# A fused forgetting-attention and SiLU block: q and k loaded in larger pieces and turned as one block, x of three more batches turned by TensorE, outputs issued by ScalarE

## Chip, cores and metric

One core of a Trainium2 chip runs the whole program. The metric is device time in microseconds (us), lower is better. Engines are named as in the profile: PE (TensorE; PEld is its weight load), DVE (VectorE), ACT (ScalarE), POOL (GpSimd), SP (SyncE, which only issues DMAs here). A q behind a name (SPq) is the engine's queue of DMA issues. Lines (L130) are those of the kernel before.

## The reference

Eight batches, eight heads, 576 tokens, head dimension 64. Attention with a forget gate, then a block of two matmuls with SiLU between them on all 4608 tokens:

```
scores = q @ k.T / sqrt(64)                       # per batch and head, 576 x 576
cum    = cumsum(log(clip(f, 1e-4, 1)))            # per batch and head
attn   = softmax(where(causal, scores + cum[i] - cum[j], -1e9))
x      = (attn @ v), heads side by side           # 4608 x 512
h      = x @ w_in                                 # 4608 x 2048
out    = (h * sigmoid(h)) @ w_out                 # 4608 x 512
```

## The kernel before

Heads go in pairs p = 0 to 31, four pairs to a batch (batch b = p // 4). For a pair the kernel needs qT and kT (head dimension on partitions, tokens along the row) and `vaug`, v scaled by the decay, which POOL prepares (`prep_v`, L246). `scores` makes the score blocks of the causal triangle in four tiles (PE `sc`, L276), ACT takes their exponential into `uT` (L301), DVE multiplies the diagonal blocks by a mask (L315). `attend_rows` multiplies uT with vaug (PE `avr`, L344), and DVE normalises the result into `xt`, token by token (L353, L354). x must then be turned so that the model dimension lies on partitions: either by PE (`turn_pair`: five transposes `tpx`, L366, and ACT copies into `xT`, L372) or by DMA transposes (`turn_batch`, L377, issued by SP).

The second half goes in nine groups of 512 tokens. `m1_chunk` makes 128 rows of h for a group (four matmuls of 128x512, PE `hp`, L395), ACT takes a tanh (L406), DVE finishes SiLU into `gtile` (L407). `m2_part` makes a quarter of an output tile of 128 tokens (four matmuls, PE `po`, L420); after the fourth ACT copies the tile to `osb` (L429), and SP issues the DMA to `out` (L433). `osb` has two buffers. All results of attention transposes, attends, hp and po share four buffers of PSUM (`big`).

How q and k get turned depends on the batch. Batches 0 and 1: loaded as float32 (`whole`, `raw`), cast by POOL (`cast_main` L188, `cast_tail` L197) and turned by PE (`transposes`, L230), copied by DVE (L235, L239). Batches 2 to 7 (`NEARLY` is 2): `load_qk` (L121) is a DMA issued by POOL that casts to bf16 on its way, one for each block of 128 tokens (the last has 64) and each of q and k, 60 in all, in pieces of 64 elements; `turn_qk` (L130) is a DMA transpose for each, issued by SP, straight into qT or kT.

The order of every engine is the order of the calls (a manual schedule). The main loop goes over pairs 4 to 31. For a pair it runs the entries of `plan` (turns and v loads, all on SP), then the scores in two halves with m1/m2 work between them (`work(n)` takes chunks off two lists, alternating where both are allowed), `prep_v` of the next pair, the casts, the entries of `fetch` (loads on POOL), and the attend of the pair before. `pace` decides how much m1/m2 work goes into a pair, so that what is ready lasts until the next group becomes ready. A group is ready when x of all its tokens is turned: for batches 0 and 1 right after the last `turn_pair`, for the later ones `LAG` (12 us of planned PE time) after the last attend, since the DMA transposes take their time. `clock`, `spend` and `defer` are that planned time.

The weights are cast-loaded by POOL as well: w_in early (L567), w_out at L611, between the casts of pair 4 and those of pair 5. In POOL's order prep_v of pair 4 (L613) follows, which needs v of batch 1.

Of the kernel before, what the change touches and what calls it, by code (L numbers as in the profile page):

```python
# [13 lines left out]
BF16 = mybir.dt.bfloat16  # L14
P = 128
# [3 lines left out]
def kernel(  # L19
# [37 lines left out]
    w_out_bf = const.tile([P, NFC, DM], BF16, name="w_out_bf")  # L57
    NVA = 3
    vaugs = [const.tile([P, NB, 2, DV], BF16, name=f"vaug{i}") for i in range(NVA)]
    kTs = [const.tile([P, NPB, NB * P], BF16, name=f"kT{i}") for i in range(2)]  # L60
    us = [const.tile([P, 2, UW], BF16, name=f"uT{i}") for i in range(3)]

    xp = ctx.enter_context(tc.tile_pool(name="xp", bufs=4))
    qkp = ctx.enter_context(tc.tile_pool(name="qkp", bufs=2))
# [6 lines left out]
    tpool = ctx.enter_context(tc.tile_pool(name="tpool", bufs=3))  # L71
    opool = ctx.enter_context(tc.tile_pool(name="opool", bufs=2))
    NEARLY = 2
    LAG = 12.0
    MOST = 9.0
    HOLD = 6
    qkT: dict[int, tuple] = {}
# [1 line left out]
    raw: dict[tuple, bass.AP] = {}  # L79

    def qk_tiles(b):
        qkT[b] = (qkp.tile([P, NPB, S], BF16, name="qT", tag="qT"), kTs[b % 2])

    def raw_tile():
        return stp.tile([P, DM], FP32, name="raw", tag="raw")
# [29 lines left out]
            in_=v[b, :, c * P : c * P + bs[c], :].rearrange("h p d -> p h d"),  # L115
        )

    def load_qk(b, c, which):
        t = sbp.tile([P, DM], BF16, name="mp", tag="mp", bufs=20)
        raw[b, c, which] = t  # L120
        nc.gpsimd.dma_start(  # L121
            out=t[: bs[c], :].rearrange("p (h d) -> p h d", h=H),
            in_=(q, k)[which][b, :, c * P : c * P + bs[c], :].rearrange("h p d -> p h d"),
        )

    def turn_qk(b, c, which):
        if b not in qkT:
            qk_tiles(b)
        n = bs[c]
        nc.sync.dma_start_transpose(  # L130
            out=qkT[b][which][:, :, c * P : c * P + n], in_=raw[b, c, which][:n, :]
        )

    f_sb = evp.tile([BH, S], FP32, name="f_sb", tag="ev")

# [278 lines left out]
    def m2_part(g, tb, part):  # L414
        if part == 0:
            po_open[g, tb] = big([P, DM], FP32, "po")
        po, gte = po_open[g, tb], gtiles[g]
        n = NFC // 4
        for fc in range(part * n, (part + 1) * n):
            nc.tensor.matmul(  # L420
                po[:, :],
                lhsT=gte[:, fc, tb * P : (tb + 1) * P],
                rhs=w_out_bf[:, fc, :],
                start=(fc == 0),
                stop=(fc == NFC - 1),
            )
        if part == 3:
            osb = opool.tile([P, DM], FP32, name="osb", tag="osb")
            nc.scalar.activation(  # L429
                out=osb[:, :], in_=po[:, :], func=ACT.Copy, scale=0.5  # L430
            )
            t0 = g * TG + tb * P
            nc.sync.dma_start(out=out[t0 : t0 + P, :], in_=osb[:, :])  # L433

    m1_queue = [(g, fc) for g in range(NG) for fc in range(NFC)]
    m2_queue = [(g, tb, pt) for g in range(NG) for tb in range(4) for pt in range(4)]
# [42 lines left out]
    def pace(p):  # L479
        b, j = divmod(p, NPB)  # L480
        if b < NEARLY:
            return have() / (NPB - j)
        for b in range(B):
            if (b + 1) * S // TG > m1_ready:
                break
        n = MOST
        for _ in range(20):
            k = NPB * b + NPB - p + LAG / (2.3 + 0.88 * n)
            n = 0.5 * n + 0.5 * have() / max(k, 1.0)
        return min(n, MOST)  # L490

# [14 lines left out]
    plan: dict[int, list] = {}  # L506

    fetch: dict[int, list] = {}

    def add(to, at, fn, *args):  # L510
        to.setdefault(at, []).append(lambda: fn(*args))

    for b in range(NEARLY, B):
        for i, group in enumerate([(0, 1), (2,), (3, 4)]):
            at = NPB * b - 4 + min(i, 1) if b == NEARLY else NPB * b - 7 + i
            for c in group:
                for w in range(2):
                    add(fetch, at, load_qk, b, c, w)
                    add(plan, at + (2 if b == NEARLY else 3), turn_qk, b, c, w)
                add(plan, NPB * b - 5 + i + (b == NEARLY), load_v, b, c, nc.sync)  # L520

    def load_w(dst, src, c0, c1):
        nc.gpsimd.dma_start(
            out=dst[:, :, c0:c1], in_=src[:, c0:c1].rearrange("(c p) x -> p c x", p=P)
        )

    with tc.manual_schedule():
# [80 lines left out]
        turn_pair(NPB - 1)  # L608
        m1_ready = 1
        cast_both(NPB)  # L610
        load_w(w_out_bf, moe_w_out, 0, DM)  # L611
        cast_both(NPB + 1)
        prep_v(NPB)  # L613
        work(HOLD)
        transposes(NPB, 0)
        work(1)
# [3 lines left out]
        for p in range(NPB, NP):  # L620
            b, j = divmod(p, NPB)
            early = b < NEARLY
            for fn in plan.get(p, []):
                fn()
            due += pace(p)
            n = int(due)
            due -= n
            n1, n2 = (n + 2) // 3, (n + 1) // 3
            n3 = n - n1 - n2
            scores(p, 0)  # L630
            scores(p, 1)
            spend(0.4)
            work(n1)
            ahead = p + 1 < NPB * NEARLY
            rows = NPB < p < NPB * NEARLY
            if ahead:
                transposes(p + 1, 0)
            if rows:
                attend_rows(p - 1, LO)
                spend(0.6)  # L640
            if p + 1 < NP:
                prep_v(p + 1)
            if p + 2 < NPB * NEARLY:
# [64 lines left out]
```

## Time and profile before

| | us |
|---|---|
| median of 3 runs (374.92, 381.12, 383.23) | 381.12 |
| the profiled execution | 378.66 |
| its span, first to last instruction | 376.9 |

| engine | busy us | share of the span |
|---|---|---|
| PE | 339.6 | 90% |
| ACT | 208.4 | 55% |
| DVE | 189.7 | 50% |
| POOL | 118.3 | 31% |

A row of the page's part 5 gives line, engine, operation, tiles out<-in, shape and count, then busy time, mean ns of one, and the idle time of the engine just before such instructions with what ended it. These are the rows of the steps that the change touches:

```profile
L121 POOL DMA_DIRECT2D mp<-in_q_dram x30 | 26.7, 889 | 0.0
L121 POOL DMA_DIRECT2D mp<-in_k_dram x30 | 25.8, 862 | 1.3 <-PE tpx L366 1.3
L372 ACT COPY xT<-tpx 128x512 bf16<-128x512 bf16 (+3 forms) x16 | 5.6, 405 | 3.6 <-PE tpx L366 3.6
```

And part 6, the DMA issues, with the size of each and the median time from issue to landing:

```profile
out_dram<-osb SPq DMA_DIRECT2D x36, 256.0 KB, 2.3
vm<-in_v_dram SPq DMA_DIRECT2D x32, 256.0 KB, 5.6
mp<-in_q_dram POOLq DMA_DIRECT2D x24, 128.0 KB, 5.1
mp<-in_k_dram POOLq DMA_DIRECT2D x24, 128.0 KB, 6.8
w_out_bf<-in_moe_w_out_dram POOLq DMA_DIRECT2D x1, 2048.0 KB, 19.0
```

KB counts the side written for a casting load. A wait row names engine, operation and line, what it waited for, the total, how often and the longest. Share of DMA in the windows can exceed 1 where several packets are under way on an engine.

### The profile page before, as it was taken

How to read it: one execution, taken by the hardware profiler on the slowest of the kernel's cores; microseconds unless marked ns; L12 is line 12 of the kernel's file. 1: busy time of each engine (PE TensorE's matmuls, PEld its weight loads, DVE VectorE, ACT ScalarE, POOL GpSimd, SP SyncE). 2: the span in 40 equal slices, each digit the busy share in tenths (PEclk: the TensorE clock that was granted, in tenths of full speed). 3: DMA queues.
4: the chain of work that ended last, by engine and by line, in shares of the span. 5: the costliest groups of instructions: out<-in, count | busy, mean ns of one | idle time of the engine just before them, and what ended most of it. 6: DMA issues, size and time to landing. Idle time of an engine off the chain costs nothing.

```text
span 376.9 us, 6954 instructions
## 1 busy us (share of the span) xinstructions
PE 339.6 (90%) x2637; PEld 165.7 (44%) x2637; DVE 189.7 (50%) x442; ACT 208.4 (55%) x329; POOL 118.3 (31%) x201
## 2 busy tenths in 40 slices
PE   2898939973999975999999999999999999999996
PEld 1455415541455442444544454444444454444442
DVE  3765844430684355775646555355535641754310
ACT  4575742532874763866566656566656723643421
POOL 5644039868045549134333421111110000000000
PEclk9999987995999998999999999999999999999999
DMA  9999988999999999969999995450310023001012
GB/s 223 221 217 289 179 174 56 132 172 143 200 167 157 138 187 181 160 82 136 156 163 151 80 138 116 105 134 28 85 64 29 30 57 92 29 0 57 28 56 83
DMA packets 152993, 46.09 MB, mean 122 GB/s; under 512 B 141120, under 2 KB 147264, under 8 KB 152960
## 3 DMA queue, kind: packets, MB, share of 16 engines
q1 hardware_dynamic: 93504, 34.23, 45.1%
q0 software_dynamic: 59376, 11.28, 40.4%
q8 instruction: 20, 0.33, 0.4%
q14 instruction: 13, 0.11, 0.1%
q10 hardware_dynamic: 80, 0.15, 0.1%
HBM read 36.85 MB, written 9.44 MB: 123 GB/s over the span
## 4 chain that ended last, share of the span: by engine, by line
PE 71%; DMA 11%; SPq 9%; POOL 4%; ACT 2%; issue 2%; DVE 1%; POOLq 0%; ACTq 0%
PE po L420 31%; PE hp L395 29%; PE sc L276 5%; PE avr L344 5%; SPq L113 4%; DMA mp<-in_k_dram 4%; DMA qT<-mp 3%; DMA vm<-in_v_dram 3%; SPq L96 2%; SPq L130 2%; POOL vaug L246 1%; ACT th L406 1%; DMA whole<-in_k_dram 1%; POOL mp L121 1%; ACT uT L301 1%
## 5 line engine op out<-in xcount | busy, mean ns | idle before, releaser
L395 PE MATMUL hp<-xT,w_in_bf 128*128 128x512 bf16 x576 | 142.8, 385 | 1.3 <-ACT xT L372 0.7
L420 PE MATMUL po<-w_out_bf,gtile 128*128 128x512 bf16 x576 | 140.8, 381 | 0.0
L407 DVE SCALAR_TENSOR_TENSOR gtile<-th,hp 128x512 bf16<-128x512 bf16 x144 | 97.4, 686 | 74.8 <-ACT th L406 71.8
L406 ACT ACTIVATE th<-hp 128x512 bf16<-128x512 f32 x144 | 85.4, 605 | 73.5 <-PE hp L395 65.5
L301 ACT ACTIVATE uT<-sc 128x1024 bf16<-128x1024 f32 (+1 forms) x128 | 100.8, 842 | 45.6 <-PE sc L276 36.7
L246 POOL TENSOR_TENSOR vaug<-vm,wT 128x512 bf16<-128x512 f32 x64 | 45.4, 730 | 147.5 <-PE avr L344 126.3
L395 PEld LDWEIGHTS <-w_in_bf 128*128 128x128 bf16 x576 | 53.8, 99 | 66.1 <-issue 7.9
L420 PEld LDWEIGHTS <-gtile 128*128 128x128 bf16 x576 | 53.8, 98 | 63.6 <-issue 3.5
L315 DVE TENSOR_TENSOR uT<-uT,mask 128x256 bf16<-128x256 bf16 (+1 forms) x112 | 34.9, 332 | 72.1 <-ACT uT L301 71.7
L276 PE MATMUL sc<-qT,kT 64*128 64x64 bf16 (+4 forms) x384 | 38.6, 293 | 17.7 <-DMA qT<-mp 10.8
L429 ACT ACTIVATE osb<-po 128x512 f32<-128x512 f32 x36 | 21.7, 602 | 39.0 <-PE po L420 32.4
L344 PE MATMUL avr<-vaug,uT 128*128 128x65 bf16 x960 | 36.5, 195 | 0.7 <-DVE uT L315 0.7
L344 PEld LDWEIGHTS <-uT 128*128 128x128 bf16 x960 | 33.9, 99 | 7.3 <-DVE uT L315 0.8
L276 PEld LDWEIGHTS <-kT 64*128 64x128 bf16 x384 | 15.3, 96 | 46.7 <-issue 32.2
L354 DVE TENSOR_TENSOR xt<-avr,rr 128x384 bf16<-128x384 f32 x64 | 31.4, 491 | 2.4
L121 POOL DMA_DIRECT2D mp<-in_q_dram x30 | 26.7, 889 | 0.0
L121 POOL DMA_DIRECT2D mp<-in_k_dram x30 | 25.8, 862 | 1.3 <-PE tpx L366 1.3
L353 DVE RECIPROCAL rr<-avr 128x6 f32<-128x6 f32 x64 | 11.6, 181 | 6.9 <-PE avr L344 6.6
L230 PE MATMUL tpqk<-ident_bf,m 128*128 128x128 bf16 (+1 forms) x70 | 9.1, 254 | 5.6 <-POOL m L188 5.4
L188 POOL CAST m<-whole 128x512 bf16<-128x512 f32 x16 | 9.6, 613 | 14.6 <-DMA whole<-in_q_dram 11.8
L230 PEld LDWEIGHTS <-m 128*128 128x128 bf16 (+1 forms) x70 | 5.7, 111 | 10.8 <-POOL m L188 5.9
L372 ACT COPY xT<-tpx 128x512 bf16<-128x512 bf16 (+3 forms) x16 | 5.6, 405 | 3.6 <-PE tpx L366 3.6
(47 smaller groups left out, 57.4 us busy)
## 6 DMA issues: line engine op xcount, KB each, us to landing
out_dram<-osb SPq DMA_DIRECT2D x36, 256.0 KB, 2.3
vm<-in_v_dram SPq DMA_DIRECT2D x32, 256.0 KB, 5.6
mp<-in_q_dram POOLq DMA_DIRECT2D x24, 128.0 KB, 5.1
mp<-in_k_dram POOLq DMA_DIRECT2D x24, 128.0 KB, 6.8
w_in_bf<-in_moe_w_in_dram POOLq DMA_DIRECT2D x2, 1024.0 KB, 11.0
w_out_bf<-in_moe_w_out_dram POOLq DMA_DIRECT2D x1, 2048.0 KB, 19.0
whole<-in_q_dram SPq DMA_DIRECT2D x3, 512.0 KB, 11.0
whole<-in_k_dram SPq DMA_DIRECT2D x3, 512.0 KB, 9.1
```

What stands on the lines that cost most here:

```text
L121: nc.gpsimd.dma_start(out=t[: bs[c], :].rearrange("p (h d) -> p h d", h=H), in_=(q, k)[which][b, :, c * P : c * P + bs[c], :].rearrange("h ...
L246: nc.gpsimd.tensor_tensor(out=va[:n, c0:c1, :, 0:D], in0=vm[:n, c0:c1, 2 * j : 2 * j + 2, :], in1=wT[:n, c0:c1, 2 * j + b * H : 2 * j + 2 ...
L276: nc.tensor.matmul(sc[:, i, col : col + n], lhsT=kT[r, kb * P : (kb + 1) * P], rhs=qT[r, q0 : q0 + n], start=True, stop=not pe_adds,)
L301: nc.scalar.activation(out=u[:, :, o : o + col], in_=sc[:, :, 0:col], func=ACT.Exp, scale=scale)
L315: nc.vector.tensor_tensor(out=d, in0=d, in1=mk, op=ALU.mult)
L344: nc.tensor.matmul(av[:, qb - lo, i, :], lhsT=u[:, i, o : o + P], rhs=va[:, kb, i, :], start=(kb == 0), stop=(kb == qb),)
L354: nc.vector.tensor_tensor(out=xt[:, lo:hi, 2 * j : 2 * j + 2, :], in0=av[:, :, :, 0:D], in1=r[:, 0:n, :, None].to_broadcast([P, n, 2, D]), ...
L395: nc.tensor.matmul(hp[:, :], lhsT=w_in_bf[:, cc, fc * P : (fc + 1) * P], rhs=xg[g][:, cc, :], start=(cc == 0), stop=(cc == NCC - 1),)
L406: nc.scalar.activation(out=th[:, :], in_=hp[:, :], func=ACT.Tanh, scale=0.5)
L407: nc.vector.scalar_tensor_tensor(out=gte[:, fc, :], in0=th[:, :], scalar=1.0, in1=hp[:, :], op0=ALU.add, op1=ALU.mult,)
L420: nc.tensor.matmul(po[:, :], lhsT=gte[:, fc, tb * P : (tb + 1) * P], rhs=w_out_bf[:, fc, :], start=(fc == 0), stop=(fc == NFC - 1),)
L429: nc.scalar.activation(out=osb[:, :], in_=po[:, :], func=ACT.Copy, scale=0.5)
```

## The change

Four things change together.

1. q and k of batches 2 to 7. A batch's q (and k) comes as one cast load of tokens 0 to 511, in which a partition holds four tokens that follow each other, 256 elements or 1 KB of float32 for each head (`mw`), and a load of the 64 last tokens (`mt`). One DMA transpose turns the 128x2048 block into `fl`, another the tail straight into qT or kT. In `fl` half of the rows are in the wrong half of the partitions and tokens stand in another order; four copies of 64 x 1024 (`spread`), two by POOL and two by DVE, put them into qT or kT. They run in the last two pairs of the batch before.
2. x of batches 2, 3 and 4 is turned by PE, as that of batches 0 and 1 (`NTURN` is 5); a group is then ready at once, and `pace` counts no lag for it. `LAG` is 10 for the others.
3. Outputs are issued by ACT in place of SP.
4. The load of w_out stands behind the casts of pair 5 and prep_v of pair 4 on POOL.

The order of PE up to the first scores of batch 2 is unchanged. Behind it, m1 chunks and m2 parts of batches 2 to 4 mostly come one after the other, where they alternated before, because only one group is ready at a time. PE has 60 transposes more.

```
@@ tiles
+    qTs = [const.tile([P, NPB, S], BF16, name=f"qT{i}") for i in range(2)]
...
-    LAG = 12.0
+    NTURN = 5
+    LAG = 10.0
...
-    def load_qk(b, c, which):
-        t = sbp.tile([P, DM], BF16, name="mp", tag="mp", bufs=20)
-        raw[b, c, which] = t
+    def load_qk(b, which):
+        src = (q, k)[which]
+        t = sbp.tile([P, H, (NB - 1) * D], BF16, name="mw", tag="mw", bufs=4)
+        e = sbp.tile([P, DM], BF16, name="mt", tag="mt", bufs=4)
+        raw[b, which] = t, e
         nc.gpsimd.dma_start(
-            out=t[: bs[c], :].rearrange("p (h d) -> p h d", h=H),
-            in_=(q, k)[which][b, :, c * P : c * P + bs[c], :].rearrange("h p d -> p h d"),
-        )
-
-    def turn_qk(b, c, which):
+            out=t[:, :, :],
+            in_=src[b, :, 0:SM, :].rearrange("h (p c) d -> p h (c d)", c=NB - 1),
+        )
+        nc.gpsimd.dma_start(
+            out=e[:TAIL, :].rearrange("p (h d) -> p h d", h=H),
+            in_=src[b, :, SM:S, :].rearrange("h p d -> p h d"),
+        )
+
+    def turn_qk(b, which):
...
-        n = bs[c]
+        t, e = raw[b, which]
+        f = sbp.tile([P, 2 * H, P], BF16, name="fl", tag="fl", bufs=3)
+        flat[b, which] = f
         nc.sync.dma_start_transpose(
-            out=qkT[b][which][:, :, c * P : c * P + n], in_=raw[b, c, which][:n, :]
-        )
+            out=f[:, :, :], in_=t.rearrange("p h x -> p (h x)")
+        )
+        nc.sync.dma_start_transpose(out=qkT[b][which][:, :, SM:S], in_=e[:TAIL, :])
+
+    def spread(b, which, i, eng):
+        h2, c2 = divmod(i, 2)
+        dst = qkT[b][which][h2 * D : (h2 + 1) * D, :, c2:SM:2].rearrange(
+            "x j (p c) -> x j c p", c=2
+        )
+        src = flat[b, which][c2 * D : (c2 + 1) * D, :, :].rearrange(
+            "x (j h c) p -> x j h c p", h=2, c=2
+        )[:, :, h2, :, :]
+        eng.tensor_copy(out=dst, in_=src)
...
-            nc.sync.dma_start(out=out[t0 : t0 + P, :], in_=osb[:, :])
+            nc.scalar.dma_start(out=out[t0 : t0 + P, :], in_=osb[:, :])
...
-            k = NPB * b + NPB - p + LAG / (2.3 + 0.88 * n)
+            k = NPB * b + NPB - p + (LAG / (2.3 + 0.88 * n) if b >= NTURN else 0)
...
     for b in range(NEARLY, B):
-        for i, group in enumerate([(0, 1), (2,), (3, 4)]):
-            at = NPB * b - 4 + min(i, 1) if b == NEARLY else NPB * b - 7 + i
-            for c in group:
-                for w in range(2):
-                    add(fetch, at, load_qk, b, c, w)
-                    add(plan, at + (2 if b == NEARLY else 3), turn_qk, b, c, w)
-                add(plan, NPB * b - 5 + i + (b == NEARLY), load_v, b, c, nc.sync)
+        at = NPB * b - (4 if b == NEARLY else 7)
+        for w in range(2):
+            add(fetch, at, load_qk, b, w)
+            add(plan, at + w + (1 if b == NEARLY else 3), turn_qk, b, w)
+            for i in range(4):
+                add(tidy, NPB * b - 1 - (i < 2), spread, b, w, i,
+                    nc.gpsimd if i in (0, 3) else nc.vector)
+        for c in range(NB):
+            add(plan, NPB * b - 5 + c // 2 + (b == NEARLY), load_v, b, c, nc.sync)
...
         cast_both(NPB)
-        load_w(w_out_bf, moe_w_out, 0, DM)
         cast_both(NPB + 1)
         prep_v(NPB)
+        load_w(w_out_bf, moe_w_out, 0, DM)
...
             for fn in fetch.get(p, []):
                 fn()
+            todo = tidy.get(p, [])
+            for fn in todo[0::2]:
+                fn()
             if early:
                 work(n2 // 2)
             scores(p, 2)
             scores(p, 3)
             spend(0.3)
+            for fn in todo[1::2]:
+                fn()
...
-            if rows:
-                work(n3)
-                n3 = 0
-                turn_pair(p - 1)
-                ready(p - 1)
-            elif b >= NEARLY and j > 0:
+            if b >= NEARLY and j > 0:
                 attend_rows(p - 1)
                 spend(1.2)
             work(n3)
+            if j > 0 and b < NTURN:
+                turn_pair(p - 1)
             if j == NPB - 1:
                 attend_rows(p)
                 spend(1.2)
-                if early:
+                if b < NTURN:
                     work(2)
                     turn_pair(p)
                     ready(p)
```

More of the change, by code (lines that the diff above doesn't have):

```diff
@@ L63 @@
     xp = ctx.enter_context(tc.tile_pool(name="xp", bufs=4))
-    qkp = ctx.enter_context(tc.tile_pool(name="qkp", bufs=2))
     vp = ctx.enter_context(tc.tile_pool(name="vp", bufs=2))
@@ L81, in qk_tiles @@
     def qk_tiles(b):
-        qkT[b] = (qkp.tile([P, NPB, S], BF16, name="qT", tag="qT"), kTs[b % 2])
+        qkT[b] = (qTs[b % 2], kTs[b % 2])
     def raw_tile():
@@ L116, in load_v @@
         )
-    def load_qk(b, c, which):
-        t = sbp.tile([P, DM], BF16, name="mp", tag="mp", bufs=20)
-        raw[b, c, which] = t
+    flat: dict[tuple, bass.AP] = {}
+    def load_qk(b, which):
[3 more added lines that the diff above has]
+        raw[b, which] = t, e
         nc.gpsimd.dma_start(
-            out=t[: bs[c], :].rearrange("p (h d) -> p h d", h=H),
-            in_=(q, k)[which][b, :, c * P : c * P + bs[c], :].rearrange("h p d -> p h d"),
-        )
-    def turn_qk(b, c, which):
+            out=t[:, :, :],
+            in_=src[b, :, 0:SM, :].rearrange("h (p c) d -> p h (c d)", c=NB - 1),
+        )
+        nc.gpsimd.dma_start(
[3 more added lines that the diff above has]
+    def turn_qk(b, which):
         if b not in qkT:
             qk_tiles(b)
-        n = bs[c]
+        t, e = raw[b, which]
+        f = sbp.tile([P, 2 * H, P], BF16, name="fl", tag="fl", bufs=3)
+        flat[b, which] = f
         nc.sync.dma_start_transpose(
-            out=qkT[b][which][:, :, c * P : c * P + n], in_=raw[b, c, which][:n, :]
+            out=f[:, :, :], in_=t.rearrange("p h x -> p (h x)")
         )
+        nc.sync.dma_start_transpose(out=qkT[b][which][:, :, SM:S], in_=e[:TAIL, :])
[8 more added lines that the diff above has]
+        eng.tensor_copy(out=dst, in_=src)
     f_sb = evp.tile([BH, S], FP32, name="f_sb", tag="ev")
@@ L508 @@
     fetch: dict[int, list] = {}
+    tidy: dict[int, list] = {}
     def add(to, at, fn, *args):
```

## The prediction, made before the changed kernel had run

> **What bounds the kernel now.** I read four views in this order. First the slices of the span: where is TensorE (PE) not full, and what is full there instead?
>
> ```profile
> PE   2898939973999975999999999999999999999996
> ...
> PEclk9999987995999998999999999999999999999999
> DMA  9999988999999999969999995450310023001012
> ```
>
> One digit is 9.4 us. From slice 17 (160 us) on PE never pauses; its holes are in the first 160 us, where the DMA row stands at 9. The windows say how much is missing:
>
> ```profile
> 40.00:60.00 20.00, 14.04 (x88) 6.06 (x88) 12.09 (x28) 10.24 (x16) 7.07 (x13) 0.85 0.90 154
> 80.00:100.00 20.00, 10.89 (x84) 4.91 (x83) 5.76 (x13) 8.49 (x16) 11.27 (x17) 0.74 1.72 177
> 120.00:140.00 20.00, 17.40 (x213) 9.42 (x212) 7.82 (x27) 13.26 (x18) 9.88 (x16) 1.00 1.39 160
> 140.00:160.00 20.00, 15.23 (x104) 6.55 (x100) 13.56 (x26) 11.62 (x20) 11.13 (x17) 0.91 1.65 167
> ```
>
> PE lacks 6.0, 9.1, 2.6 and 4.8 us there, and after an idle stretch its granted clock is down (0.85, 0.74, 0.91). Third, what ended PE's waits:
>
> ```profile
> PE sc L276 <- DMA qT<-mp: 10.8, 4, 3.7
> PE tpqk L230 <- POOL m L188: 5.4, 1, 5.4
> PE sc L276 <- ACT uT L301: 4.1, 8, 0.9
> PE tpx L366 <- ACT osb L429: 2.3, 1, 2.3
> ```
>
> The first is the turned q/k of batches 2 and 3; the second is the cast of pair 6, stuck in POOL's queue; the fourth is an output tile that waits for its DMA. The timeline shows batch 2's case (the last transposes that SP issues, and PE):
>
> ```profile
> 83.59 1.20 SPq L130 DMA_TRANSPOSE qT<-mp  x1
> 84.90 1.19 SPq L130 DMA_TRANSPOSE kT<-mp  x1
> ...
> 87.53 0.61 PE L276 MATMUL sc<-qT,kT 64*128 64x512 bf16 x2 [3.11 <-DMA qT<-mp]
> ...
> 91.81 0.61 PE L276 MATMUL sc<-qT,kT 64*128 64x64 bf16 x4 [3.67 <-DMA qT<-mp]
> ...
> 92.36 3.09 PE L395 MATMUL hp<-xT,w_in_bf 128*128 128x512 bf16 x8
> ```
>
> Eight warm matmuls take 1.90 us elsewhere (99.84), so the stall also cost 1.2 us of slow clock. Last, the DMA queues while w_out loads (36 to 40 us):
>
> ```profile
> q0 software_dynamic: 530, 0.54, 100.2%
> q1 hardware_dynamic: 221, 0.06, 8.1%
> ```
>
> w_out takes the engines, and batch 1's v creeps; prep_v(4) then holds POOL's queue for 16.6 us, and behind it the cast for which PE waits 5.4 us.
>
> So the kernel is PE's work plus the stalls of the first 160 us. The profiled execution took 378.66 us (span 376.9, 1.76 around it); the median of the three runs, 381.12, is 2.5 above. I add up changes of the span.
>
> **What the change takes away.** PE's order is the same up to the first scores of batch 2 (pair 8), so stalls can be compared one by one.
> - Wait for qT at pair 8: 3.11 + 3.67 + 1.2 of clock = 8.0.
> - Outputs leave SP for ACT: the osb tile that waited 5.08 us for its DMA (SP was busy with transposes) frees earlier, and tpx's wait of 2.3 goes.
> - Pairs 9 to 12, where x of batch 2 came late and little PE work was ready: 0.32 + 0.33 (hp on gtile), 0.52 + 0.90 + 0.52 + 0.52 (sc on exponentials), 0.71, 1.55 + 2.50 (qT of batch 3), and 4.03 − 2.76 = 1.3 of clock for twelve hp: 9.2. With x turned by PE the m1 chunks of batches 2 to 4 stand directly behind each batch.
> Together 19.5.
>
> **What it adds or moves.**
> - *w_out behind prep_v(4).* Without w_out, batch 1's v keeps the 1.14 MB in 4 us that its queue had at 32 to 36 us: the 0.9 MB that the queue moved between 36 and 52 us (batch 2's first v in it) takes some 3 us, and v is there near 40. prep_v(4) lasts 1.5, so w_out is issued at 41.5. It landed 19.0 us after issue beside v; at w_in's rate (0.79 MB in 4 us) 2 MB take 10.6, with the same 4.6 around it 15.2. I take 17: 58.5. PE is ready for its first po at 52 and now waits for w_out, where it waited for the cast before; that po ran at 58.17, so +0.3 (−2.7 to +2.3). The same wait as before, with another cause.
> - *q/k of batch 2.* They queue behind w_out (drained near 57). The pieces are larger, but the rows show no faster cast load for it: mp's 128-byte pieces reach 154 to 165 GB/s written, w_out's 1 KB pieces 0.63 MB in 4 us (157), w_in's 2 KB pieces 197. So 1.18 MB take 6 to 7.6 us, and q's main block lands near 61.6. The Trainium skill ("DMA: Bandwidth & Descriptors", Specifications) says that pieces under 512 B pay a read-modify-write, by which the new loads would be quicker; the mp row does not show it. By the rule the 2.5 us of pair 6 below would go, and the time be 369.0.
> - *Turning.* 60 + 33 transposes of 1.2 us on SP become 24 + 17. The 128x2048 block has no row. A 128x512 took 1.22 and a 64x512 1.19, so cost doesn't go with rows; both have four column blocks, the new one sixteen: 1.2 if per instruction, 4.9 if per block. I take 3.4, nearer the block count. Then: q's block 61.6 to 65.0, its tail to 66.2, two v loads to 67.5, k's block to 70.9, landed at 72.5 (a transpose lands 1.2 after its issue ends in quiet, 6.4 under load; I take 1.6).
> - *Copies into order.* 48, half on DVE, half on POOL, 64 x 1024 each. DVE: L235 (512 elements, 0.685) and L239 (64, 0.18) give 1.26; as low as 0.85 by L315 (512 in 0.425). POOL: L188 gives 1.0, L246 2.1. Both engines have the time (DVE 50% busy, POOL 31% with 52 us of issues of which some 20 stay). They cost only where something queues behind them: in pair 6, DVE's copy of k stands before the kT copy of pair 7 (due at 70.9) and two normalisations. Waiting for 72.5, it ends at 73.8, the rest 1.3 later, and tpx, due at 72.7, starts at 75.2: **+2.5**. For later batches the blocks are loaded seven pairs ahead: nothing.
> - A row bears on copies side by side: a mask multiply (L315) of 0.29 took 2.07 at 144.9, while POOL issued loads and ran L246. The Trainium skill ("SBUF — State Buffer", Who interferes with whom) has DVE and POOL lock each other out of a shared port in two-input and fast copy operations; the row agrees. By it pair 6's copies would go one by one, 1.2 more, and the time be 372.7.
> - *PE turns.* 12 pairs x 5 transposes, 0.32 to 0.45 a pair by the distance to the next instruction (72.60 to 72.92, 80.05 to 80.50): 4.8 at 0.40. At the end of batches 2, 3 and 4 nothing stands between the last attend and its turn: PE idles while DVE normalises (81.07 to 82.40, less the attend under it), 0.83 each: 2.5. ACT's 24 copies of 0.41 lie beside PE.
> - *Light pairs.* m1/m2 work runs out at pairs 25 and 26 as it did at pairs 10 to 12 (2.46 over three): 1.6. m1-only stretches: 0.65 as in pairs 9 and 10.
> - *36 output issues on ACT*, 0.34 each: 12 us on an engine that is 55% busy; nothing. Each also waits for the hardware DMA eight before it; the third for k's block of batch 2, when it is due anyway.
>
> Sum: −19.5 + 0.3 + 2.5 + 4.8 + 2.5 + 1.6 + 0.65 = −7.15: span 369.75, time **371.5**.
>
> **Rivals.**
> - *Quick turning* (0.20): issue cost per instruction, w_out at w_in's rate. No stall in pair 6, w_out −2.7, turns 3.8, no light pairs: −19.5 − 2.7 + 3.8 + 2.5 = −15.9, time 362.8. For it: 64 and 128 rows cost the same. Against: w_out's own 135 to 157 GB/s.
> - *The load is no sooner and DVE blocks* (0.18): the pieces bring nothing. w_out lands after 19.0 (+2.3), loads at 155, 4.9 per block, landing 6.4 later since batch 3's loads are on the queue: q lands at 63.9, k's block is issued by 76.2 and there at 82.6; DVE's copy ends at 83.9, tpx starts at 85.2 where 74.7 was due: 10.5 and 1.3 of clock. In place of 0.3 + 2.5 that is 14.1: time 382.8, level. For it: landings of 7 to 8 us at 76 to 100.
> - *ACT becomes the bound by its issues* (0.12, slower). On SP some output issues took 1.44, 2.31 and 4.80 right behind transposes. On ACT the exponentials and xT copies queue behind such an issue, and PE behind them. A pair of m2 work costs PE 32 x 0.216 + 2.4 = 9.3, ACT 3.2 (exponentials) + 0.9 (xT) + 1.2 (osb) + two issues: it decides from 2.0 us an issue. At 3.4 six such pairs (10, 11, 14, 15, 18, 19) cost 2.8 each: +17, time 388. Against: the median issue is 0.344.
>
> **Numbers.** The first case has 0.50, its own range 367 to 377. Two per cent is about what three runs of 374.92 to 383.23 can tell; the cut is 371.1 from the profiled run, 373.5 from the median, so I give 0.30 of it to faster, 0.20 to the same. With quick turning (0.20) and 0.02 of the DVE case faster is 0.52; the same 0.20 + 0.12 = 0.32; slower 0.12 + 0.04 = 0.16. The range 362 to 386 leaves out the ACT case.
>
> **What would show it.** Right: no wait of sc for qT at pair 8; the first po waits for w_out until 56 to 61; in pair 6 DVE waits for the turned k and tpx for DVE; PE full from pair 8 on but for some tenths per batch end. Wrong: block transposes far from 3.4 on SP; copies over 2 us; output issues over 2 us on ACT, with exponentials late; PE gaps inside batches 3 and 4.

## The result and the profile after

The changed kernel is slower by 6%: 400.01 us (median of four runs, 398.97 to 402.63) against 380.56 for the kernel before beside it (four runs); the ratio is 1.061, 95% interval 1.046 to 1.076. That ratio compares fast executions alone, and two of the four of the kernel before (381.12 and 383.23) were slow, so it is above 400.01 / 380.56 = 1.051. The profiled execution took 399.21 us, span 397.4: 20.5 more than before. Lines are now those of the changed kernel (copies L154, masks L337, normalisation L376, turns by PE L388, hp L417, gtile L429, po L442).

The busy slices first (one digit is 9.9 us now):

```profile
PE   2898949277999899989998959866999999999996
...
DVE  4765934166887588758875895289845551464410
...
PEclk9999989869999999999999998998999999999999
```

PE's holes of 120 to 160 us are gone; a deeper one stands at 70 to 100 us, and new ones from 220 to 280 us, where before it was full. In the last of these DVE reads 8 and 9. The windows:

```profile
60.00:80.00 20.00, 12.05 (x117) 6.49 (x115) 6.07 (x16) 5.70 (x10) 5.48 (x5) 0.93 1.36 188
80.00:100.00 20.00, 15.88 (x134) 7.88 (x135) 12.50 (x22) 9.25 (x17) 17.57 (x16) 0.81 0.87 148
140.00:160.00 20.00, 20.00 (x163) 9.88 (x162) 16.94 (x31) 14.53 (x26) 6.55 (x6) 1.00 0.66 110
```

From 140 to 160 us PE had lacked 4.8 us; now nothing. From 60 to 100 it lacks 12.1 (9.1 before, all of it from 80 to 100). Where the list of waits named transfers, it now mostly names DVE (some of its rows):

```profile
PE tpx L388 <- DVE xt L376: 16.8, 17, 9.9
PE po L442 <- DMA w_out_bf<-in_moe_w_out_dram: 5.2, 1, 5.2
PE hp L417 <- DVE xt L376: 4.1, 1, 4.1
PE po L442 <- DVE gtile L429: 3.8, 1, 3.8
PE avr L366 <- DVE gtile L429: 2.0, 2, 1.8
```

No wait of sc for a turned q is left. The timeline of pair 6 shows the longest wait of all, the 9.9 us of tpx. It comes from the order of DVE's queue:

```profile
59.78 5.34 SPq L141 DMA_TRANSPOSE fl<-mw  x1
...
70.42 6.58 SPq L141 DMA_TRANSPOSE fl<-mw  x1
...
74.05 1.30 DVE L154 COPY qT<-fl 64x1024 bf16<-64x1024 bf16 x1 [4.25 <-DMA fl<-mw]
...
79.49 1.29 DVE L154 COPY kT<-fl 64x1024 bf16<-64x1024 bf16 x1 [4.14 <-DMA fl<-mw]
...
81.99 0.45 PE L388 MATMUL tpx<-ident_bf,xt 128*128 128x128 bf16 x2 [9.94 <-DVE xt L376]
```

SP issued q's block in 5.3 us and k's in 6.6. DVE stood still until the one had landed, copied, stood still for the other, copied, and only then normalised x of pair 5, for which PE waited 9.9 us. The next eight matmuls took 3.60 us in place of 1.90 (granted clock 0.81 in the window from 80 to 100).

What the copies do elsewhere is in the groups by line. The first row is that of the kernel before, the others are those of the changed kernel:

```profile
L315 DVE TENSOR_TENSOR uT<-uT,mask 128x256 bf16<-128x256 bf16 (+1 forms) x112 | 34.9, 332 | 72.1 <-ACT uT L301 71.7
...
L337 DVE TENSOR_TENSOR uT<-uT,mask 128x256 bf16<-128x256 bf16 (+1 forms) x112 | 55.2, 519 | 61.1 <-ACT uT L323 60.3
...
L154 DVE COPY kT<-fl 64x1024 bf16<-64x1024 bf16 x12 | 17.8, 1485 | 4.1 <-DMA fl<-mw 4.1
...
L154 POOL COPY kT<-fl 64x1024 bf16<-64x1024 bf16 x12 | 31.1, 2592 | 1.9 <-DMA fl<-mw 1.9
```

With the rows for qT, DVE's 24 copies come to 34.9 us and GpSimd's to 61.7. The masks, the same 112 instructions, grew from 34.9 us (mean 332 ns) to 55.2 (519). The 0.66 us that the expectations below name is the mean of the 128x256 masks alone.

### The profile page after: what moved, and what is told of

Its sections match the earlier page's. It is cut to its first block, busy times and chain, and to the rows that moved or that the text cites. A ratio compares the mean times of both kernels' runs of the same rounds, so it can differ in the third digit from the quotient of the medians.

```text
span 397.4 us, 6933 instructions
## 1 busy us (share of the span) xinstructions
PE 347.9 (88%) x2697; PEld 170.7 (43%) x2697; DVE 239.6 (60%) x466; ACT 215.0 (54%) x353; POOL 152.9 (38%) x189
## 4 chain that ended last, share of the span: by engine, by line
PE 67%; DVE 16%; DMA 7%; ACT 5%; issue 2%; SPq 1%; POOL 1%; ACTq 0%; POOLq 0%; DVEq 0%
PE hp L417 27%; PE po L442 26%; PE sc L298 6%; DVE uT L337 5%; PE avr L366 5%; DMA w_out_bf<-in_moe_w_out_dram 4%; DVE kT L154 3%; ACT uT L323 3%; DVE xt L376 3%; DVE qT L154 3%; DMA fl<-mw 2%; PE tpx L388 2%; DVE gtile L429 1%; DMA whole<-in_k_dram 1%; PE tpqk L252 1%
## 5 line engine op out<-in xcount | busy, mean ns | idle before, releaser
L442 PE MATMUL po<-w_out_bf,gtile 128*128 128x512 bf16 x576 | 140.4, 388 | 8.9 <-DMA w_out_bf<-in_moe_w_out_dram 5.2
L417 PE MATMUL hp<-xT,w_in_bf 128*128 128x512 bf16 x576 | 138.3, 383 | 5.1 <-DVE xt L376 4.1
L429 DVE SCALAR_TENSOR_TENSOR gtile<-th,hp 128x512 bf16<-128x512 bf16 x144 | 95.3, 685 | 51.5 <-ACT th L428 47.3
L268 POOL TENSOR_TENSOR vaug<-vm,wT 128x512 bf16<-128x512 f32 x64 | 49.8, 799 | 115.5 <-PE avr L366 110.5
L337 DVE TENSOR_TENSOR uT<-uT,mask 128x256 bf16<-128x256 bf16 (+1 forms) x112 | 55.2, 519 | 61.1 <-ACT uT L323 60.3
L442 PEld LDWEIGHTS <-gtile 128*128 128x128 bf16 x576 | 54.3, 99 | 74.0 <-issue 10.1
L417 PEld LDWEIGHTS <-w_in_bf 128*128 128x128 bf16 x576 | 53.7, 98 | 69.5 <-issue 6.3
L154 POOL COPY qT<-fl 64x1024 bf16<-64x1024 bf16 x12 | 30.6, 2554 | 11.9 <-DMA fl<-mw 11.5
L376 DVE TENSOR_TENSOR xt<-avr,rr 128x384 bf16<-128x384 f32 x64 | 31.4, 491 | 2.3
L154 POOL COPY kT<-fl 64x1024 bf16<-64x1024 bf16 x12 | 31.1, 2592 | 1.9 <-DMA fl<-mw 1.9
L394 ACT COPY xT<-tpx 128x320 bf16<-128x320 bf16 (+7 forms) x40 | 14.0, 404 | 26.1 <-PE tpx L388 24.4
L388 PE MATMUL tpx<-ident_bf,xt 128*128 128x128 bf16 (+1 forms) x100 | 12.6, 219 | 16.8 <-DVE xt L376 16.8
L154 DVE COPY kT<-fl 64x1024 bf16<-64x1024 bf16 x12 | 17.8, 1485 | 4.1 <-DMA fl<-mw 4.1
L154 DVE COPY qT<-fl 64x1024 bf16<-64x1024 bf16 x12 | 17.1, 1421 | 4.5 <-DMA fl<-mw 4.3
L388 PEld LDWEIGHTS <-xt 128*128 128x128 bf16 (+1 forms) x100 | 7.9, 96 | 24.7 <-DVE xt L376 20.9
## 6 DMA issues: line engine op xcount, KB each, us to landing
w_out_bf<-in_moe_w_out_dram POOLq DMA_DIRECT2D x1, 2048.0 KB, 15.6
```

The source lines that it names most:

```text
L154: eng.tensor_copy(out=dst, in_=src)
L268: nc.gpsimd.tensor_tensor(out=va[:n, c0:c1, :, 0:D], in0=vm[:n, c0:c1, 2 * j : 2 * j + 2, :], in1=wT[:n, c0:c1, 2 * j + b * H : 2 * j + 2 ...
L337: nc.vector.tensor_tensor(out=d, in0=d, in1=mk, op=ALU.mult)
L376: nc.vector.tensor_tensor(out=xt[:, lo:hi, 2 * j : 2 * j + 2, :], in0=av[:, :, :, 0:D], in1=r[:, 0:n, :, None].to_broadcast([P, n, 2, D]), ...
L388: nc.tensor.transpose(tp[:, c * P : c * P + n], xtok[b][:n, c, 2 * j : 2 * j + 2, :].rearrange("p h d -> p (h d)"), ident_bf[:n, :n],)
L417: nc.tensor.matmul(hp[:, :], lhsT=w_in_bf[:, cc, fc * P : (fc + 1) * P], rhs=xg[g][:, cc, :], start=(cc == 0), stop=(cc == NCC - 1),)
```

## The experiments

Each was timed beside the kernel before, whose median there was 379.5 to 381.3 us; times are medians of four to ten executions, ratios are to the kernel before, with the 95% interval. "Delay" is the start of DVE's last normalisation of a pair (L376) against the same instruction of another run: PE's order of work is the same in runs that differ only in the copies, so the pair at which a delay grows is where time is lost.

**Which part of the change carries the loss.** Theory: the copies. Rivals: the turns by PE and the order they force; the outputs on ACT; a stall in pair 6 that only covers another.

Old loads and turns of q and k, everything else as changed:

```
-    def load_qk(b, which): ...      # mw, mt, fl, spread
+    def load_qk(b, c, which): ...   # mp, as before
-            add(tidy, ...)
```

> The changed kernel with q/k of batches 2 to 7 loaded in the old small pieces and turned straight into place by SP: no block transposes, no copies; x turned by PE, outputs on ACT and w_out behind prep_v stay. Theory (the copies on DVE and GpSimd hold PE: the stall of pair 6, 9.9 + 1.7 us of slow clock, and the 13.0 us of idle PE between 220 and 280 us with 3 us of slow clock): both go, a wait of sc for the turned q at pair 8 comes back (6.8 to 8 us), so from 399.2 to 399.2 - 11.6 - 16 + 8 = about 380, no PE gap over 1 us from 220 us on. Rival (the lost time is the PE turns and the stretches of pure m1 or m2 work): at least 392, with gaps from 220 us on as now.

Measured: 379.18 us, ratio 0.996 (0.992 to 1.000). The other three parts together are worth next to nothing without the new loads; the whole loss comes with the new way of q and k.

x of batches 2 to 4 turned by DMA again:

```
-    NTURN = 5
-    LAG = 10.0
+    NTURN = 2
+    LAG = 12.0
```

> The changed kernel with x of batches 2 to 4 turned by SP again, the lag back at 12 us. Theory (copies): the turns (4.8) and the waits of tpx at the ends of batches 2 to 4 (4.2) go, waits for late x take their place (the kernel before had 4.8 at such places), the stall of pair 6 and the gaps behind copies stay: 392 to 400. Rival (x turned by PE and the order it forces): most of the 20 us return, 385 or less, and DVE's copies stand beside a PE that never waits for them.

Measured: 420.58 us (416.38 to 424.38), 1.110 (1.099 to 1.120). Neither theory expected it: the turns by PE are no loss; beside the copies they save some 20 us. They are taken up again below.

Outputs by SP again:

```
-            nc.scalar.dma_start(out=out[t0 : t0 + P, :], in_=osb[:, :])
+            nc.sync.dma_start(out=out[t0 : t0 + P, :], in_=osb[:, :])
```

> The changed kernel with the outputs issued by SP again. Theory (outputs are no part of the loss except where an output issue in pair 6 stood behind a transfer): the issue on ACT at 77 us goes, exponentials of pair 6 and 7 run earlier, but tpx still waits for DVE and for copies; osb tiles wait behind block transposes of 5 to 6 us: 396 to 404. Rival (ACT held by its issues): 392 or less.

Measured: 401.80 us, 1.057 (1.051 to 1.063). Not the outputs.

Batch 2's copies a pair later:

```
-                add(tidy, NPB * b - 1 - (i < 2), spread, b, w, i,
+                add(tidy, NPB * b - 1 - (i < 2 and b > NEARLY), spread, b, w, i,
```

> The changed kernel with batch 2's eight copies all in pair 7, none in pair 6; other batches as now. Theory: the 9.9 us wait of tpx for the normalisation in pair 6 and its 1.7 us of slow clock go; k's block lands near 79 us, four DVE copies of 1.3 stand in pair 7 and cost 2 to 5: 390 to 394. Rival (PE turns and pure stretches carry the loss; the stall of pair 6 only shifts a later wait): 397 to 400.

Measured: 402.53 us, 1.059 (1.053 to 1.066). The theory missed, and the time came out above the rival's range as well. The wait for k's block was gone, but in its place PE waited 3.5 us for exponentials, because an output issue held ACT until 77.5 (see *Outputs on ACT* below), and in pair 7 four copies, two masks that took 4.52 us together (0.55 elsewhere) and a last copy of 3.64 beside GpSimd's copies held DVE from 81.5 to 93.2 us, so that tpx waited 8.2.

**Queue or lock.** The Trainium skill ("SBUF — State Buffer", Who interferes with whom) says that a DVE operation with two SBUF inputs and a GpSimd one that reads SBUF exclude each other for a whole instruction, and that ACT waits for nobody. If that is the loss, the copies should go to one engine.

All copies on DVE; all on GpSimd; GpSimd's half on ACT:

```
-                    nc.gpsimd if i in (0, 3) else nc.vector)
+                    nc.vector)                                    # first run
+                    nc.gpsimd)                                    # second
+                    nc.scalar if i in (0, 3) else nc.vector)      # third
```

> The changed kernel with all 48 ordering copies on DVE, none on GpSimd. DVE gets 24 copies of 1.3 us more (31 us). If GpSimd's copies hurt by locking DVE out (mask multiply 0.66 us on the mean, 0.33 before the change): masks back to 0.33 to 0.40, copies at 1.3, the idle PE from 220 to 280 us falls from 13 to 9 or less, 394 to 398. If it is only the work in DVE's queue: masks come back but the gaps from 220 us on grow to 16 or more, 402 or more. The stall of pair 6 stays near 10 or grows by the two further copies (2.6) in either case.

> The changed kernel with all 48 ordering copies on GpSimd (2.5 us each, 120 us there), none on DVE. If what hurts is what stands in DVE's own queue ahead of masks and normalisations: the wait of tpx in pair 6 (9.9) and the gaps from 220 to 280 us (13.0) go, 375 to 386, with perhaps a new wait for GpSimd's copies of batch 2 before pair 8 (eight of 2.5 us from 74 to 94 us, against 96 now). If what hurts is GpSimd locking DVE out: the mask multiply goes above its 0.66 us, to 0.9 or more on the mean, gaps from 220 us on stay at 8 us or more, 392 or more.

> The changed kernel with GpSimd's 24 copies given to ACT; DVE keeps its own 24. No GpSimd copy can lock DVE. If the lock carries the gaps from 220 to 280 us: masks back at 0.33 to 0.40, DVE's copies at 1.3, those gaps from 13.0 to 5 or less, 384 to 391 (less if ACT's copies are short, more if the stall of pair 6, which now holds ACT too, grows). If it is the copies' place in DVE's queue: the gaps stay at 9 or more, 394 or more. An ACT copy of 64x1024 has no row so far: 1.0 to 1.5 us by the xT copies (512 columns in about 0.5).

Measured: 413.54 us, 1.088 (1.081 to 1.095); 405.86, 1.065 (1.061 to 1.069); 434.90, 1.142 (1.135 to 1.149). Mean mask: 353, 759 and 329 ns. So the lock is there as the skill has it (GpSimd's copies stretch the masks, ACT's don't), but 48 copies on DVE without it cost more than 24 with it. With all on GpSimd, PE waits twice for the last copies of a batch, 13.9 us in all, and the masks are longest. An ACT copy took 2.5 us, not the 1.0 to 1.5 of the expectation, and PE's longest wait was now one for ACT (16.6 us of tpx for osb), so the third run doesn't decide on the lock's price.

**Leaving copies out.** No copies, one engine's half alone, all but batch 2's:

```
-                add(tidy, NPB * b - 1 - (i < 2), spread, b, w, i, ...)
+                pass                                              # first run
+                if i in (1, 2): add(tidy, ...)                    # second: DVE's alone
+                if i in (0, 3): add(tidy, ...)                    # third: GpSimd's alone
+                if b > NEARLY: add(tidy, ...)                     # fourth
```

> The changed kernel without the 48 ordering copies: batches 2 to 7 then compute with the order that batches 0 and 1 left in qT and kT; loads, block transposes, turns and outputs stay. If the copies alone are the loss: no wait of tpx in pair 6, no gaps over 1 us from 220 to 256 us, masks at 0.33; left are the turns (4.8), the batch ends (4.2) and light pairs of some 5: 399.2 - 11.6 - 13 + 1 = 372 to 378. If the block transposes and loads cost too (SP held 5 to 7 us, DMA queues): 382 or more.

> The changed kernel with DVE's 24 copies alone; GpSimd's 24 are left out, so half of each turned block is not put in order. DVE's queue is as in the changed kernel, but nothing locks it out: masks at 0.33, copies at 1.3, DVE's work 20 us less. If the lock is half or more of the loss from 220 us on: gaps from 220 to 280 us at 6 or less (13.0 now), 386 to 392. If DVE's queue is the loss: gaps at 9 or more, 393 to 399. The wait of pair 6 stays (8 to 10) in both.

> The changed kernel with GpSimd's 24 copies alone; DVE's 24 are left out. Masks stay long where they meet a copy (0.5 to 0.66 on the mean), but no copy stands in DVE's queue. If DVE's queue is the loss: wait of tpx in pair 6 gone, gaps from 220 us on under 5, 376 to 384. If the lock is: gaps at 7 or more, 386 to 394.

> The changed kernel with the eight copies of batch 2 alone left out (it computes with batch 0's order). It prices pair 6: the wait of 9.9 and 1.7 of slow clock, and the copies of 1.3 to 2.2 in pair 7, against the wait for the turned tails that remains. Theory: 399.2 - 12 = 386 to 389. If that stall only covers another (an output issue on ACT that stood to 77.3 behind a transfer, as when the copies were put one pair later, 402.5): 393 to 399.

Measured: 373.61 us, 0.986 (0.983 to 0.990); 390.40, 1.031 (1.028 to 1.034); 379.58, 0.999 (0.995 to 1.004); 393.42, 1.040 (1.035 to 1.045). That settles the part: without copies the change is a gain, and the copies cost 26.4 us: DVE's alone 16.8, GpSimd's alone 6.0, and 3.6 more when both are there. The second run's time lay in the range given for the lock, but PE's idle time from 220 to 280 us (10.3) in that given for DVE's queue, so that run alone doesn't part the two. Batch 2's copies are worth 6.6 (400.0 - 393.4), not the 12 of the theory: their stall covers another, as its rival had it. Where the delay arises (us against the run without copies, at the last normalisation of each batch):

| end of batch | copies in the batch are for | changed | DVE's alone | GpSimd's alone |
|---|---|---|---|---|
| 1 | batch 2 | 8.4 | 8.5 | 1.2 |
| 2 | batch 3 | 9.5 | 8.5 | 1.2 |
| 3 | batch 4 | 10.6 | 8.6 | 1.2 |
| 4 | batch 5 | 11.9 | 8.5 | 1.2 |
| 5 | batch 6 | 17.6 | 13.7 | 1.8 |
| 6 | batch 7 | 25.6 | 16.9 | 4.9 |

Copies of the same length cost 8.5 in batch 1, nothing in batches 2 to 4, and 5.2 and 3.2 in batches 5 and 6 (DVE's alone). Batch 1 is the wait for the blocks. What parts the others shows in the run without copies: windows over the two halves of batch 3, and over the pairs that would copy for batches 6 and 7:

```profile
126.00:144.00 18.00, 17.84 (x128) 8.39 (x127) 13.73 (x28) 15.66 (x29) 4.93 (x9) 1.00 0.68 97
144.00:162.00 18.00, 17.89 (x171) 9.60 (x172) 4.94 (x17) 8.81 (x14) 3.14 (x6) 1.00 0.56 143
215.50:232.00 16.50, 16.02 (x167) 8.49 (x170) 9.55 (x26) 10.11 (x16) 3.70 (x7) 1.00 0.52 115
243.00:259.00 16.00, 14.55 (x157) 8.08 (x159) 12.57 (x32) 12.59 (x20) 5.75 (x12) 1.00 0.09 26
```

After the length come the busy times of PE, PEld and DVE. Where PE turns x itself, the first half of a batch is m1 work (a gtile of 0.685 us on DVE for every chunk) and the second half m2 work, which needs no DVE: DVE has 13.7 and 4.9 us of 18. The copies stand in the second half: 4.9 and four copies of 1.3 are 10.1 of 18, and they are free. From batch 5 on DMAs turn x again and m1 work falls into the last pairs. For batch 7, 12.6 and 5.2 are 17.8 of 16, more than there is, before any lock. For batch 6, 9.6 and 5.2 are 14.8 of 16.5, which would go in, and yet the copies cost 5.2: with DVE's copies alone PE stood 3.9 us before its next po, waiting for a gtile that stood behind two masks and two copies. So a stretch need not be full; it is enough that m1 work comes behind the copies and PE waits for it. In the changed kernel, the first 16 us of the pairs that copy for batch 7; window, then timeline:

```profile
261.00:277.00 16.00, 10.24 (x85) 4.86 (x85) 15.22 (x18) 9.03 (x15) 13.88 (x9) 0.89 0.06 21
```

```profile
261.37 2.47 POOL L154 COPY qT<-fl 64x1024 bf16<-64x1024 bf16 x1
261.99 5.35 DVE L337 TENSOR_TENSOR uT<-uT,mask 128x256 bf16<-128x256 bf16 x3 [0.62 <-ACT uT L323]
263.65 2.48 POOL L154 COPY kT<-fl 64x1024 bf16<-64x1024 bf16 x1
267.37 1.40 DVE L154 COPY qT<-fl 64x1024 bf16<-64x1024 bf16 x1
268.58 1.32 DVE L154 COPY kT<-fl 64x1024 bf16<-64x1024 bf16 x1
...
270.57 1.04 PE L417 MATMUL hp<-xT,w_in_bf 128*128 128x512 bf16 x4 [4.14 <-DVE xt L376]
```

Three masks of some 0.3 us each took 5.35 us while GpSimd copied, two copies followed, then the normalisation. DVE was busy 15.2 of 16 us, PE 10.2.

**The place of the copies.** If what stands right behind a copy in DVE's queue makes it dear, another place in the pair must help; if it is the m1 work of the whole stretch, it must not. DVE's two at the end of the pair; all 48 on DVE, one at a time at four places; and, for batches 4 to 7, one on each engine in every pair:

```
+    tail: dict[int, list] = {}                  # first run: DVE's copies
...
             work(n3)
+            for fn in tail.get(p, []):
+                fn()
```

```
+            turn = iter(tidy.get(p, []))        # second run, at four places of a pair
+            for fn in turn:
+                fn()
+                break
```

```
-        at = NPB * b - (4 if b == NEARLY else 7)
+        at = NPB * b - (4 if b == NEARLY else 7 if b == NEARLY + 1 else 8)
...
-                add(tidy, NPB * b - 1 - (i < 2), spread, b, w, i,
+                add(tidy, NPB * b - 1 - (i < 2) - (2 * (1 - w) if b > NEARLY + 1 else 0), spread, b, w, i,
```

> The changed kernel with DVE's two copies of a pair put behind the pair's scores, attends and m1/m2 work (ahead of the turn of the pair before); GpSimd's stay where they are. If the place in DVE's queue carries the loss (a copy of 1.3 us ahead of the gtile and normalisation that PE needs next): the 3.8 us wait of po for gtile at 237 us and the waits of 4.1 and 1.8 at 264 to 280 us shrink to 1 to 2 each, 389 to 395; pair 6 stays or grows. If the amount of DVE work does: 397 or more.

> All 48 copies on DVE as in the run with 413.5 us, but one by one at four places of a pair instead of two by two; same amount of work, no lock. If place counts: 403 or less, no wait for gtile over 3 us from 220 us on. If amount counts (DVE has 4 x 1.3 us more in a pair of about 9.4): 408 to 416. Pair 6 and 7 cost some 10 to 12 in both, since the copies stand behind blocks that land at 74 and 79 us.

> The changed kernel with the copies of batches 4 to 7 spread over four pairs: one on DVE and one on GpSimd in every pair in place of two and two in two pairs of four (loads and turns of these batches one pair sooner); same copies, same engines, same total. If what holds PE is that the work of DVE in the pairs with copies (17.8 us busy of the 18.0 from 262 to 280) is more than these pairs take on PE: the gaps from 220 to 280 us (13.0 with the short ones) fall to 5 or less, 386 to 392; left are pair 6 and 7 (8.4) and batch 3. If it is the total of the copies wherever they stand: 396 or more.

Measured: 412.26 us, 1.086 (1.074 to 1.098); 409.27, 1.080 (1.069 to 1.091); 402.07, 1.059 (1.054 to 1.065). No other place within a pair helped (in the first run GpSimd's copies in the last pair of a batch also stand earlier): there the waits moved to the next scores (2.9 for a copy, 3.4 for vaug) and to another gtile (5.7). The third has the time that was expected of a total that costs the same wherever it stands, but its delays don't bear that out: they grow by 2.5 in batch 3, 3.3 in batch 4, 5.1 in batch 5 and 4.7 in batch 6, where the changed kernel has 1.1, 1.4, 5.7 and 8.0. Spreading took copies out of the crowded pairs of batch 6 and put others into the m1 halves that had been spared. In batches 3 to 5 nearly all of the growth falls in the first two pairs, those with the m1 work, and PE's new waits there are for a gtile (0.8 to 2.1 us each); in batch 6 the longest is one of 3.5 us for a normalisation behind masks and a copy. So what a copy costs goes largely by the m1 work that it meets, and evenly spread about half of them meet it.

**The turns by PE, by themselves.** The run without copies, with x of batches 2 to 4 by DMA:

```
-    NTURN = 5
-    LAG = 10.0
+    NTURN = 2
+    LAG = 12.0
```

> The version without copies, with x of batches 2 to 4 turned by SP's DMAs and the lag at 12 us, as before the change. It prices the turning of x by itself, free of copies. By the prediction's sum (9.2 gained; 4.8 + 2.5 + 1.6 + 0.65 paid) it is level with 373.6: 371 to 377. If turning by DMA is worth far less, as the 420.6 with copies suggests: 381 or more.

Measured: 375.42 us, 0.988 (0.983 to 0.992), beside 0.986 (0.983 to 0.990) with the turns by PE: level. With DMAs turning x, the 48 copies cost 45 us by the medians (420.6 against 375.4) and 41 in the profiled executions, and the delay between these two runs grows in every batch: 7.6, 14.0, 25.3, 30.4, 35.8, 40.9 at the ends of batches 1 to 6. PE's waits there are many and mixed (11.3 of hp for gtile, 12.3 of tpx, 6.0 of avr for masks); m1 and m2 work mostly alternate there, so hardly a pair is free of m1 work. That agrees with the reading above and again shows that a stretch need not be full: from 238.7 to 262.8 us of the run without copies DVE was busy 13.3 of 24.1 us, DVE's four copies for batch 7 would make it 18.5, and DVE's and GpSimd's together cost 5 us there. Why the whole is some 40 to 45 us and not 26 was not traced further.

**A version that beats both.** Old q and k, and step by step: outputs on SP with four tiles of osb and a lag of 14; w_out in four row blocks; x of all batches turned by PE.

```
-    opool = ctx.enter_context(tc.tile_pool(name="opool", bufs=2))
+    opool = ctx.enter_context(tc.tile_pool(name="opool", bufs=4))
...
-        load_w(w_out_bf, moe_w_out, 0, DM)
+        for c0 in range(0, NFC, NFC // 4):      # second and third run
+            nc.gpsimd.dma_start(
+                out=w_out_bf[:, c0 : c0 + NFC // 4, :],
+                in_=moe_w_out[c0 * P : (c0 + NFC // 4) * P, :].rearrange("(c p) x -> p c x", p=P),
+            )
...
-    NTURN = 5
+    NTURN = 8                                   # third run
```

> The kernel with q/k the old way, x of batches 2 to 4 turned by PE and w_out behind prep_v, with three edits against the 379.2 us of that version: outputs on SP again with four output tiles in place of two (ACT waited 4.8 us with an output issue behind the turned k in pair 6, PE 2.8 + 1 of slow clock), and the lag of the batches that DMAs turn at 14 us in place of 10 (light pairs between 242 and 254 us: 0.9 + 0.5 + 0.5 + 2.7 and 1.5 of slow clock). If both readings hold: 379.2 - 3 to 4 - 4 to 6 = 369 to 372. If the waits only shift (qT at pair 8 late again): 375 to 380.

> The 377.5 us version (old q/k, x of batches 2 to 4 turned by PE, w_out behind prep_v, four output tiles, lag 14) with w_out loaded as four row blocks instead of one: the first quarter of an output tile needs the first block alone. PE waits 5.9 us for w_out now. If the blocks land one after the other: that wait falls to 1 to 3, but what stands behind it (the fourth quarter, then the turned q at pair 8) takes part of it back: 373 to 376. If they land together or the next wait takes it all: 377 to 378.

> The 376.5 us version with x of all batches turned by PE: no transposes of x on SP, no lag, no light pairs. Gone: 2.8 (turned q of batch 7 late behind x on SP), some 3.5 of light pairs between 234 and 247 us, 1 of slow clock. Paid: 12 turns of 0.40 = 4.8 and three batch ends of 0.55. Sum -0.9: 374 to 377. If m1 work of the last batches then stands in stretches that DVE bounds: 378 or more.

Measured: 377.47 us, 0.991 (0.987 to 0.994); 376.54, 0.993 (0.989 to 0.997); 372.67, 0.981 (0.977 to 0.985). The first fell short: part of the waits only shifted. The row blocks took PE's wait of 5.9 us for w_out off the list, but waits for turned q grew from 4.2 to 7.7, so little came of it. With all x turned by PE the time came out below the range of 374 to 377, and PE is full from 90 us on:

```profile
PE   2798989949999999999999999999999999999995
...
DVE  3764884416823683268425842484248524743410
```

DVE's digits swing with m1 and m2 (8 and 2) in every batch. This version beats the changed kernel, and the one before by 1.9%.

## Why the prediction was wrong

- *What is taken away* was right in kind: the wait of sc for the turned q and that of tpx for osb are gone from the list of waits, and PE is nearly full in pairs 9 to 12 (18.7 of 20 us from 120 to 140).
- *w_out* was right in its course: prep_v ended, w_out was issued at 41.47 (41.5 forecast), and PE waited for it. It landed 15.6 us later rather than 17, and the first po ran at 57.11, 1.06 sooner than before where 0.3 later was forecast. The lower bound of -2.7 doesn't follow from its own figures: 41.5 + 15.2 - 58.17 is -1.5. The rival with quick turning uses it and leaves out the 0.65 of m1-only stretches; with both put right it would be 364.6, not 362.8.
- *Turns, batch ends, light pairs* (a net +0.35): with DMAs in their place, and no copies, the time is level (375.42 against 373.61).
- *Outputs on ACT, nothing*: right for the issue (0.34 to 0.36) and in the changed kernel (401.8 without it). The wait that the prediction named was not harmless, and it was the second issue that met it: without copies that issue stood from 70.8 to 76.3 us, until a load of v had landed at 76.2 that uses the same completion semaphore. PE waited 2.64 for exponentials, and its next eight po took 3.62 in place of 1.90. In the changed kernel the stall of pair 6 covers it.
- *Turning*: 3.4 a block against a mean of 3.65 over the twelve, but the two for batch 2 took 5.34 and 6.58, above the upper bound of 4.9, with a DMA share of 1.55 and 1.39 meanwhile. The last one, with a share of 0.73, took 1.63. That the load on the DMA engines makes the issue long is not shown by these three alone.
- *Pair 6*: the mechanism was forecast as it came (DVE's copy waits for k's block, tpx for DVE), 2.5 us; it was 9.9 and 1.7 of slow clock, 8.4 net. k's block was there at 79.5, not 72.5. Q's block left SP when it was forecast (65.1), so the 7 us came behind it: the two v loads in between took 3.8 us to issue where 1.3 was put, k's block 6.6 for 3.4, and it landed 2.4 after that for 1.6. The rival in which DVE blocks (10.5 and 1.3) had the size, partly by luck, since the load was not the reason: q's block was already being turned at 59.8.
- **The step that failed** is the one on the copies: "Both engines have the time (DVE 50% busy, POOL 31% ...)", and "For later batches the blocks are loaded seven pairs ahead: nothing." A DVE copy by itself was priced well (1.26 against 1.30), a GpSimd one too low (2.1 at most against 2.5). But 50%, which DVE has without copies as well (187.6 of 371.8), is a mean over stretches of 76% and 27%, and the copies for batches 6 and 7 stood in stretches with m1 work, for which PE waits. Of the 25.6 us, 8.4 came from pair 6, 13.7 from batches 5 and 6, and 3.5 from batches 2 to 4, where DVE's copies alone cost nothing. So the term was +2.5 where the runs have +26.4. Without that term the sum was -9.65; the run without copies gave -5.8 (0.983 to 0.990). The 2.64 and 1.7 that the output issue cost there are of the size of that difference; the other terms were not traced one by one.
- *The lock* was seen at one row (2.07 for 0.29) and priced for pair 6 alone, at 1.2. GpSimd's copies add 20 us to DVE's masks; in time they cost 6.0 alone and 9.6 beside DVE's (400.0 against 390.4).

New loads and block transposes by themselves saved 5.6 us by the medians (379.18 to 373.61) and 3.7 by the ratios to the kernel before (0.996 to 0.986), of the 8.0 forecast for the wait at pair 8. Not tried: the changed kernel with x of all batches turned by PE, where all copies from batch 3 on would stand in m2 halves.

## What to carry to other kernels

Before work is put on an engine "that has the time", read its busy share in the very stretch where the work will stand, with the other work of that stretch in it; a mean over the kernel hides halves of 76% and 27%. On an in-order engine that feeds the bound engine, ask also what stands behind the added instruction and how soon the bound engine wants it: here added copies were free where DVE came to 56%, cost their whole length at 90%, and were not free at 77% either where each pair had work that PE waited for. To price an addition, leave it out and compare the same instruction's start in both traces: the point where the delay grows is the place of the cost.

## What the runs showed of the hardware

- A copy of 64 x 1024 bf16 with these strides took 1.30 us on DVE, 2.47 on GpSimd and 2.5 on ACT.
- A mask multiply on DVE: mean 327 ns without copies, 348 beside DVE's own, 516 with 24 on GpSimd, 759 with 48, 329 with 24 on ACT; the longest was 4.03 us, for a usual 0.29.
- The issue of one 128x2048 DMA transpose on SP took from 1.63 to 6.58 us in the changed kernel, one of 128x512 1.2 us in the kernel before.
- DMAs issued by SP and ACT share eight completion semaphores in turn (in the trace of the kernel before, each bears that of the one eight before it). An output issue on ACT stood 5.5 us without copies, and 6.5 in the changed kernel, until a load of v that SP had issued with the same semaphore had landed (76.20 and 77.23; the issues began at 76.27 and 77.31).
